# Sparse attention into a two-layer network: the local scores of batches 4 to 7 as one group in six PSUM banks

## The chip, the cores and the metric

The kernel runs on one core of a Trainium2 chip. The metric is device time in microseconds, the median of several executions. Five engines matter here: TensorE (PE, matrix products and transposes into PSUM), ScalarE (ACT: exponentials, relu, copies out of PSUM), VectorE (DVE: masks, squares, normalising), GpSimd (POOL, which here mostly issues loads that cast from fp32 to bf16) and SyncE (SP, which issues the output DMAs and the transposes done by DMA).

## The reference

Attention over 8 batches, 8 heads, 576 positions and 64 channels, with two masks, followed by a network of two layers on all 4608 tokens:

```
mask_local   = (rel >= 0) & (rel < 32)                              # heads 0 to 3
mask_strided = (rel >= 0) & (pos[None, :] % 32 == pos[:, None] % 32) # heads 4 to 7
scores = where(masks, q @ k.T / sqrt(64), -1e9)
attn   = softmax(scores);  x = (attn @ v) as 4608 tokens x 512
out    = relu(x @ w_in) ** 2 @ w_out        # 512 -> 2048 -> 512
```

## The kernel before, in words

**The dense part** is a list of 288 groups of four TensorE products with 512 columns each. The tokens are cut into 9 chunks of 512, and chunk c has groups 32c to 32c+31. The first 16 groups of a chunk are the first layer (`mm1`, L671): ACT's relu takes each result out of PSUM (L685), and DVE squares it (L686). The other 16 are the second layer (`mm2`, L690): four groups fill one output block y, ACT copies it out (L705), and SP sends it. In chunk 0 the second layer goes through w_out quarter by quarter, and its four blocks stay open side by side.

**The attention** is woven between the groups by hand. `PLAN` is a table: a line `n: words` says which steps are issued just before group n (L909 on). Each engine works through its own instructions in the order in which they were issued, so the table sets the order on every engine. Units are numbered u = 4 x batch + pair of heads; units 4b and 4b+1 are the local heads of batch b. The steps that matter below:

- `Su` (`step_S`, L470): the scores of local unit u, 12 small products of 64 rows by 96 columns, in pairs for the two heads of the unit (rows 0 to 63 and 64 to 127 of the array). They fill four half banks of PSUM with 288 columns each, and ACT takes four exponentials of them (L516). With `!` the exponentials are issued at once; otherwise they are spread over the following groups by `later`. DVE then multiplies by the mask (L522).
- `Du.p` (`step_D`, L630): the weighted sums of head p of unit u, six products, then a reciprocal and a multiplication on DVE (L644, L645).
- `Eu` (`step_E`, L649): puts the result x of unit u in its transposed place in `xt`, the input of the first layer. For batches 0 and 1 it uses six TensorE transposes (L661) and a copy (L664) by ACT (`a`) or DVE (`v`); from batch 2 on SP does it with a DMA (L654).
- `sb.p` and `xb.p` (`step_SS`, L539; `step_XX`, L552): part p (0, 1, 2) of the scores and of the products of the strided heads of batch b. An x step takes two banks: one for the sums (L557), of which ACT takes Ln and Exp (L562, L563), and one for the product (L560), which DVE multiplies into `xt` (six instructions at L570 for parts 0 and 1, four at L576 for part 2).
- `Cbq`, `Cbk` load the rows of the strided heads (L354, POOL), `Xbq`, `Xbk` transpose them by DMA (L359, SP), and `kb..` (L370, L373) and `Bb..` (L402) spread keys and values into block form on DVE.
- `Quk`, `Quq` load the rows of a local unit (L283, POOL), `Yu` transposes them by DMA (L383, SP: queries `qT`, then keys `kTl`), `Vb` and `Ub` load values (POOL). In batches 2 and 3 the local queries and keys are cast (`c..`) and transposed by TensorE (`T..`).

**PSUM** has eight banks. Two (`ph`) take the first layer and the second layer of all chunks but the first. One (`py`) is used by chunk 0 alone. Five (`pt`) form a ring that the attention steps take in turn: `bank("pt")` pops the first and puts it at the end. A step that is handed a bank must wait until its last user's result has been read. During groups 19 to 31 one of the five is lent to an output block of chunk 0.

```
    banks = {"ph": [all_banks[i] for i in (4, 5)], "py": [all_banks[2]],
             "pt": [all_banks[i] for i in (6, 7, 0, 1, 3)]}
...
        t = banks[nm].pop(0)
        banks[nm].append(t)
```

Of the kernel before, what the change touches and what calls it, by code (L numbers as in the profile page):

```python
# [9 lines left out]
BF16 = mybir.dt.bfloat16  # L10
AF = mybir.ActivationFunctionType
ALU = mybir.AluOpType
# [28 lines left out]
22: l3k12+13 s1.2  # L41
23: D5.1 x1.0
24: E4a
25: E5a x1.1
26: X2k l3q12+13
27: x1.2
28: V3
29: c9kv
30: c8qv
31: c8ka c9qv X2q  # L50
# [34 lines left out]
77: s3.2  # L85
80: x3.0 B40v
81: B41v
83: x3.1
89: x3.2
90: k40v  # L90
91: S16! k41v
95: U5 D16.0 D16.1
96: S17
97: Y20
99: X5k
100: C6k
# [5 lines left out]
106: Q25k  # L102
107: B50v
108: s4.2 D17.1 B51v
109: Q24k Q24q
111: E17
113: k50v
114: k51v
116: x4.0
119: x4.1  # L110
124: V6
125: x4.2
128: U6 S20!
130: S21
133: D20.0
134: Y24 D20.1 X6k
135: E20 X6q s5.0 C7q Q28k
# [4 lines left out]
141: B60v  # L122
142: E21
143: B61v
148: x5.0
150: x5.1 k60v
152: k61v
153: x5.2
155: S24!
156: V7  # L130
157: U7
161: S25
162: D24.0
165: s6.0 D24.1
166: s6.1
167: X7q
171: X7k
172: B70v
173: Y28 B71v
174: E24 D25.0 D25.1  # L140
175: x6.0 Y29
178: E25
179: s6.2
182: x6.1
186: x6.2
188: k70v
189: k71v
191: S28!
192: S29
197: s7.0  # L150
198: D28.0 s7.1
199: D29.0
# [10 lines left out]
def kernel(  # L163
# [9 lines left out]
    nc = tc.nc  # L173
    B, H, S, D = q.shape
# [4 lines left out]
    scale = 1.0 / (D ** 0.5)  # L179
    QL = 96  # L180
    NL = S // QL
# [12 lines left out]
    singles = ctx.enter_context(tc.tile_pool(name="singles", bufs=1))  # L194
# [15 lines left out]
    banks = {"ph": [all_banks[i] for i in (4, 5)], "py": [all_banks[2]],  # L210
             "pt": [all_banks[i] for i in (6, 7, 0, 1, 3)]}
    places = []

    def bank(nm):
        if places:
            return all_banks[places.pop(0)]
        t = banks[nm].pop(0)
        banks[nm].append(t)
        while id(t) in unread:
            run_due(lambda x: x[1] == unread[id(t)])  # L220
        return t
# [13 lines left out]
    mask_all = singles.tile([128, NL, QL], BF16)  # L235
# [7 lines left out]
    mask_bd = singles.tile([128, 1, W3], BF16)  # L243
    str_rows_t = {nm: singles.tile([SR, RW], BF16, name=f"{nm}_t") for nm in "qk"}
    kTl = [singles.tile([128, 32 + S], BF16, name=f"kTl{i}") for i in range(NV)]
    es = [singles.tile([128, 1280], BF16, name=f"e{i}") for i in range(4)]
    xt = [singles.tile([128, T], BF16, name=f"xt{p}") for p in range(4)]
    w_in_b = singles.tile([128, 4, d_ff], BF16)
    w_out_b = singles.tile([128, 16, d_model], BF16)
# [14 lines left out]
    st = {}  # L264
# [34 lines left out]
    def cast_qk_local(u, name, copy):  # L299
        s = st[u]  # L300
        t = qk_in.tile([QL, 6, 2, D], BF16, name=f"{name}_l")
        copy(t.rearrange("p j h d -> p h j d"), s[name + "f"].rearrange("p h (j d) -> p h j d", j=6))
        s[name] = t
# [62 lines left out]
    def step_K(b, par, copy):  # L366
        o = str_T[b, "k"]
        r = slice(64 * par, 64 * par + 64)
        kb = kbds[b % 2][r, :, 64 * par:64 * par + W3]
        copy(kb[:, 0:NP2], o[r, 0:NP2, 0:W3])  # L370
        src = o[r, :, W3:SP_]
        src = bass.AP(src.tensor, src.offset, [src.ap[0], [SR, NG + 1], [NG * SR, 3], [1, NA]])
        copy(kb[:, NP2:NB].rearrange("c n (g m) -> c n g m", g=3), src)  # L373
# [64 lines left out]
    def later(n, fn, key=None):  # L438
        pending.append((clock[0] + n, key, fn))

    def run_due(test):
        due = [x for x in pending if test(x)]
        for x in due:
            pending.remove(x)
        for x in sorted(due, key=lambda x: x[0]):
            x[2]()
# [5 lines left out]
    def step_T(u, name, copy):  # L452
        s = st[u]
        src = s[name].rearrange("p j h d -> p (j h d)")
        pt = bank("pt").bitcast(BF16)[:, 0:S]
        for j in range(6):
            nc.tensor.transpose(pt[:, QL * j:QL * (j + 1)], src[:, 128 * j:128 * (j + 1)],  # L457
                                ident[0:QL, 0:QL])
        if name == "k":
            full = kTl[v_slot(u)]  # L460
            dst = full[:, 32:32 + S]
        else:
            full = dst = qkT.tile([128, S], BF16, name="qT")
        copy(dst.rearrange("c (p j) -> c p j", j=6), pt.rearrange("c (j p) -> c p j", j=6))
        s[name + "T"] = full
# [4 lines left out]
    def step_S(u, mode=0, halves=range(2)):  # L470
# [48 lines left out]
        def masks(row):  # L519
            x = e[0:kn, S * row:S * (row + 1)].rearrange("p (t c) -> p t c", c=w)  # L520
            m = mask_all if local else mask_str.to_broadcast([kn, n, w])
            nc.vector.tensor_tensor(x, x, m, op=ALU.mult)  # L522
# [10 lines left out]
        later(3, lambda: expo(1, 1), u)  # L533
        later(4, lambda: masks(1), u)

    def blocks(part):
        return range(NJ * part, min(NJ * (part + 1), NB))

# [89 lines left out]
                                r.to_broadcast([QL, 2, NL, D]), op=ALU.mult)  # L628

    def step_D(u, part):  # L630
        run_due(lambda x: x[1] == u)
        s = st[u]
        e = s["e"]
        rhs = s["v"].rearrange("p h t d -> p (h t) d")
        po = bank("pt")[:, 0:NL * (D + 1)].rearrange("p (n d) -> p n d", d=D + 1)
        for n in range(NL):
            c = QL * (NL * part + n)
            m = QL if (part, n) == (0, NL - 1) else 128
            nc.tensor.matmul(po[0:m, n, :], e[:, c:c + m], rhs[:, NL * part + n, 0:D + 1], start=True, stop=True)  # L639
        if part == 0:  # L640
            s["x"] = xl_pool.tile([QL, 2 * NL, D], BF16, name="x_l")
        x = s["x"].rearrange("p (t h) d -> p h t d", h=2)[:, part]
        rinv = small.tile([128, NL, 1], FP32, name="rinv")
        nc.vector.reciprocal(rinv[0:QL], po[0:QL, :, D:D + 1])  # L644
        nc.vector.tensor_tensor(x, po[0:QL, :, 0:D], rinv[0:QL].to_broadcast([QL, NL, D]), op=ALU.mult)  # L645
# [66 lines left out]
    A, V, G = nc.scalar.copy, nc.vector.tensor_copy, nc.gpsimd.tensor_copy  # L712
# [19 lines left out]
    def warm(n):  # L732
        if n:
            pw = bank("py")
            for _ in range(n):
                nc.tensor.matmul(pw, idle[:, 0:128], idle, start=True, stop=True)
# [7 lines left out]
    def run_step(word):  # L744
        word, _, at = word.partition("/")
        places[:] = [int(x) for x in at.split(",") if x]
        op, arg = word[0], word[1:]
        if op == "w":
            warm(int(arg))
        elif op == "c":  # L750
            cast_qk_local(int(arg[:-2]), arg[-2], ENG[arg[-1]])
        elif op == "T":
            step_T(int(arg[:-2]), arg[-2], ENG[arg[-1]])
        elif op == "W":
            step_TS(int(arg[0]), arg[1], int(arg[2]), ENG[arg[3]])
        elif op == "S":
            u, _, half = arg.rstrip("!").partition(".")
            step_S(int(u), int("!" in arg), [int(half)] if half else range(2))
        elif op == "N":
            step_N(int(arg))  # L760
        elif op == "O":
            step_O(int(arg))
        elif op in "sx":
            (step_SS if op == "s" else step_XX)(*(int(x) for x in arg.split(".")))
        elif op == "k":
            step_K(int(arg[0]), int(arg[1]), ENG[arg[2]])
        elif op == "m":
            memset_later(arg[:-1], nc.gpsimd if arg[-1] == "g" else nc.vector)
        elif op == "D":
            if "." in arg:  # L770
                u, part = arg.split(".")
                step_D(int(u), int(part))
            else:
                step_D0(int(arg))
        elif op == "E":
            step_E(int(arg.rstrip("av")), ENG.get(arg[-1]))
        elif op == "P":
            first_part([int(x) for x in arg])
        elif op == "H":
            shift_v_local(int(arg[:-1]), ENG[arg[-1]])  # L780
        elif op == "C":
            load_str_tall(int(arg[:-1]), arg[-1])
        elif op == "Q":
            load_qk_rows(int(arg[:-1]), arg[-1])
        elif op == "X":
            transpose_str(int(arg[:-1]), arg[-1])
        elif op == "Y":
            transpose_local(int(arg))
        elif op == "V":
            load_v_local_all(int(arg))  # L790
        elif op == "U":
            load_v_str(int(arg))
        elif op == "B":
            spread_v_str(int(arg[0]), int(arg[1]), ENG[arg[2]])
        elif op == "l":
            load_qk_local_sw(int(arg[0]), [int(x) for x in arg[2:].split("+")], arg[1])
        elif op == "r":
            load_str_rows(int(arg[0]), arg[1])
        elif op == "i":
            load_w_in(int(arg))  # L800
        elif op == "o":
            load_w_out(int(arg))
        elif op == "z":
            late_constants()
        else:
            raise ValueError(word)
# [99 lines left out]
    for line in PLAN.strip().splitlines():  # L906
        n, words = line.split(":")
        plan.setdefault(int(n), []).extend(words.split())
    for n, g in enumerate(groups):  # L909
        for word in plan.get(n, ()):  # L910
            run_step(word)
        g()
        tick()
# [32 lines left out]
```

## Time and profile before

| | us |
|---|---|
| median of 3 runs | 302.91 (302.55 to 303.26) |
| the profiled execution | 302.61 |
| its span, first to last instruction | 300.9 |
| TensorE matmuls busy | 291.6 |
| VectorE busy | 178.6 |
| ScalarE busy | 173.2 |

Times of events are microseconds from the start of the span. A "busy" TensorE is not TensorE at its peak: products overlap, so one product of 512 columns is listed with 379 ns, but four in a row take 0.86 us. Some records of products are missing, so counts such as x15 can stand for 16. The granted clock of TensorE is 1.000 over the whole span. "L560 <- L570" in a wait means that line 560's instruction waited for line 570's. A DMA's time to landing is counted from its issue.

### The profile page before, as it was taken

The page shows a single profiled execution, that of the slowest core. Times are in us where ns is not written, and L with a number is a line of the kernel's source. Part 1 is how long each engine was busy: PE and PEld are TensorE (multiplying, and loading weights), DVE is VectorE, ACT ScalarE, POOL GpSimd, SP SyncE. Part 2 cuts the span into 40 slices and gives each one's busy share as a digit, 9 for nine tenths or more (in the row PEclk, how much of TensorE's full clock was granted, in tenths as well). Part 3 has the DMA queues.
Part 4 walks back from the last instruction along what each step waited for, and adds up shares of the span by engine and source line. Part 5 has one row for each costly group of instructions (what it writes and reads, how often), then busy time and mean ns, then how long its engine had stood idle before and what let it go on. Part 6 is the DMA issues. An engine that isn't in the chain of part 4 may idle for free.

```text
span 300.9 us, 5686 instructions
## 1 busy us (share of the span) xinstructions
PE 291.6 (97%) x2141; PEld 146.2 (49%) x2179; DVE 178.6 (59%) x459; ACT 173.2 (58%) x332; POOL 72.1 (24%) x105
## 2 busy tenths in 40 slices
PE   7989998999999999999999999999999999999996
PEld 3644554545545444444454445444454444444444
DVE  5776688588679677585467485666575524104400
ACT  3777855786668734874387447643875356226611
POOL 8755932007204009064302820000000000000000
PEclk9999999999999999999999999999999999999999
DMA  7999999997999999999998999511011110010012
GB/s 153 179 207 202 189 203 190 166 215 114 142 169 158 149 155 197 150 160 119 208 157 153 151 195 164 84 55 71 35 23 25 68 68 1 35 72 35 0 70 72
DMA packets 93643, 37.28 MB, mean 124 GB/s; under 512 B 78956, under 2 KB 87750, under 8 KB 93616
## 3 DMA queue, kind: packets, MB, share of 16 engines
q0 software_dynamic: 54960, 18.82, 59.2%
q1 hardware_dynamic: 38512, 18.03, 32.4%
q8 instruction: 17, 0.28, 0.4%
q10 hardware_dynamic: 144, 0.07, 0.1%
q14 instruction: 10, 0.08, 0.1%
HBM read 38.21 MB, written 9.44 MB: 158 GB/s over the span
## 4 chain that ended last, share of the span: by engine, by line
PE 84%; DMA 9%; POOL 3%; issue 2%; DVE 1%; ACT 0%; DVEq 0%; POOLq 0%
PE psb L701 38%; PE psb L679 37%; DMA w_in_b<-in_moe_w_in_dram 5%; DMA w_out_b<-in_moe_w_out_dram 4%; PE psb L639 2%; PE psb L500 1%; PE psb L560 1%; PE psb L546 1%; PE psb L726 1%; PE psb L557 1%; DVE xt L570 1%; POOL w_in_b L429 1%; PE psb L457 1%; POOL xt L295 0%; POOL vl L423 0%
## 5 line engine op out<-in xcount | busy, mean ns | idle before, releaser
L679 PE MATMUL psb<-xt,w_in_b 128*128 128x512 bf16 x557 | 131.8, 379 | 1.3 <-DMA w_in_b<-in_moe_w_in_dram 0.2
L701 PE MATMUL psb<-w_out_b,g_sb 128*128 128x512 bf16 x542 | 126.1, 379 | 1.4 <-issue 0.5
L685 ACT ACTIVATE r<-psb 128x512 bf16<-128x512 f32 x144 | 85.9, 599 | 34.2 <-PE psb L679 31.0
L686 DVE TENSOR_TENSOR g_sb<-r 128x512 bf16<-128x512 bf16 x144 | 60.3, 424 | 65.2 <-ACT r L685 64.5
L679 PEld LDWEIGHTS <-w_in_b 128*128 128x128 bf16 x576 | 53.1, 98 | 58.7 <-issue 1.0
L701 PEld LDWEIGHTS <-g_sb 128*128 128x128 bf16 x560 | 51.7, 97 | 57.5 <-DVE g_sb L686 0.5
L705 ACT COPY y<-psb 128x512 f32<-128x512 f32 x35 | 20.6, 590 | 53.2 <-PE psb L701 50.4
L570 DVE TENSOR_TENSOR xt<-psb,rv 64x144 bf16<-64x144 f32 x84 | 33.9, 404 | 18.2 <-ACT rv L563 17.1
L516 ACT ACTIVATE e<-psb 128x288 bf16<-128x288 f32 x56 | 19.9, 416 | 6.7 <-PE psb L500 6.7
L562 ACT ACTIVATE rv<-psb 128x432 f32<-128x432 f32 (+1 forms) x21 | 10.5, 502 | 12.2 <-PE psb L557 12.2
L576 DVE TENSOR_TENSOR xt<-psb,rv 64x270 bf16<-64x270 f32 (+1 forms) x28 | 10.9, 432 | 8.8 <-ACT rv L563 8.6
L645 DVE TENSOR_TENSOR x_l<-psb,rinv 96x384 bf16<-96x384 f32 x28 | 15.5, 553 | 1.0
L522 DVE TENSOR_TENSOR e<-e,mask_all 128x576 bf16<-128x576 bf16 x28 | 12.4, 452 | 3.8 <-ACT e L516 3.5
L547 ACT ACTIVATE e<-psb 128x432 bf16<-128x432 f32 (+1 forms) x21 | 10.4, 496 | 6.0 <-PE psb L546 6.0
L354 POOL DMA_DIRECT2D q_t<-in_q_dram x6 | 3.4, 575 | 41.8 <-DMA qT_s<-q_t 27.8
L423 POOL DMA_DIRECT2D vl<-in_v_dram x7 | 10.0, 1435 | 10.7 <-DMA vl<-in_v_dram 6.7
L283 POOL DMA_DIRECT2D q_l<-in_q_dram x16 | 11.6, 732 | 3.9 <-DMA k_t<-in_k_dram 1.9
L283 POOL DMA_DIRECT2D k_l<-in_k_dram x16 | 11.8, 741 | 2.7 <-DMA k_t<-in_k_dram 1.4
L563 ACT ACTIVATE rv<-rv 128x432 f32<-128x432 f32 (+1 forms) x21 | 11.2, 533 | 0.7
L639 PEld LDWEIGHTS <-e 128*128 128x128 bf16 x168 | 8.4, 100 | 4.8
L354 POOL DMA_DIRECT2D k_t<-in_k_dram x6 | 3.3, 546 | 27.5 <-DMA kT_s<-k_t 27.2
L560 PEld LDWEIGHTS <-vb 128*128 128x128 bf16 x154 | 7.1, 97 | 5.0 <-issue 1.3
(114 smaller groups left out, 209.2 us busy)
## 6 DMA issues: line engine op xcount, KB each, us to landing
out_dram<-y SPq DMA_DIRECT2D x35, 256.0 KB, 4.4
vl<-in_v_dram POOLq DMA_DIRECT2D x7, 384.0 KB, 12.2
w_in_b<-in_moe_w_in_dram POOLq DMA_DIRECT2D x4, 512.0 KB, 12.3
w_out_b<-in_moe_w_out_dram POOLq DMA_DIRECT2D x4, 512.0 KB, 13.3
q_t<-in_q_dram POOLq DMA_DIRECT2D x7, 288.0 KB, 5.8
k_t<-in_k_dram POOLq DMA_DIRECT2D x7, 288.0 KB, 7.1
v_st<-in_v_dram POOLq DMA_DIRECT2D x7, 216.0 KB, 8.4
k_l<-in_k_dram POOLq DMA_DIRECT2D x16, 72.0 KB, 8.7
```

The source lines that it names most:

```text
L283: nc.gpsimd.dma_start(out=t[:, :, hh, :], in_=src[b, 2 * p + hh].rearrange("(t p) d -> p t d", p=QL))
L516: nc.scalar.activation(e[0:kn, lo:lo + S // 2], pss[row][half][0:kn, 0:S // 2], AF.Exp, scale=scale)
L522: nc.vector.tensor_tensor(x, x, m, op=ALU.mult)
L563: nc.scalar.activation(rv, rv, AF.Exp, scale=-1.0)
L570: nc.vector.tensor_tensor(to[:, :, NJ * part:NJ * (part + 1), par], of, by, op=ALU.mult)
L639: nc.tensor.matmul(po[0:m, n, :], e[:, c:c + m], rhs[:, NL * part + n, 0:D + 1], start=True, stop=True)
L645: nc.vector.tensor_tensor(x, po[0:QL, :, 0:D], rinv[0:QL].to_broadcast([QL, NL, D]), op=ALU.mult)
L679: nc.tensor.matmul(ph, w_in_b[:, kk, 128 * ff:128 * (ff + 1)], xt[kk][:, 512 * c:512 * (c + 1)], start=(kk == order[0]), stop=(kk == order ...
L685: nc.scalar.activation(r, ph, AF.Relu)
L686: later(1, lambda: nc.vector.tensor_tensor(g[:, ff, :], r, r, op=ALU.mult))
L701: nc.tensor.matmul(py, g[:, ff, 128 * j:128 * (j + 1)], w_out_b[:, ff, :], start=(ff == 0), stop=(ff == 15))
L705: nc.scalar.copy(y, py)
```

## The change

1. **Early.** `E5a`, the transposition of x of unit 5 (batch 1) with ACT's copy, is issued before group 28 instead of group 25, after `V3`. Before group 25 then stands `x1.1` alone.
2. **Six banks.** From group 32 on, the bank of `py` joins the ring of the attention steps, which then has six.
3. **Batches 4 to 7.** A new step `Gb` takes the place of the two steps `S(4b)` and `S(4b+1)`. It issues the 24 score products of both local units in one go, into six banks with 384 columns each (three banks for either head of the pair), and at once six exponentials of 384 columns. The four masks follow two and three groups later. The two tiles `e0` and `e1` become halves of one tile, ordered by head, then unit. `G4` to `G7` stand before groups 90, 121, 154 and 188, all in the second layer of a chunk; the S steps stood before 91 and 96, 128 and 130, 155 and 161, 191 and 192.
4. **Strided products.** The x steps of batches 3 to 6 move so that they are done before the G step: x3.1 and x3.2 from 83 and 89 to 82 and 85; x4 from 116, 119, 125 to 109, 112, 116; x5 from 148, 150, 153 to 144, 146, 149; s6.2 from 179 to 169; x6.1 and x6.2 from 182 and 186 to 179 and 183.
5. **D** reads the new order, and its last weights of part 1 are 96 columns wide instead of 128 in batches 4 to 7.

```diff
-25: E5a x1.1
+25: x1.1
 26: X2k l3q12+13
 27: x1.2
-28: V3
+28: V3 E5a
...
-83: x3.1
-89: x3.2
-90: k40v
-91: S16! k41v
+82: x3.1
+85: x3.2
+90: G4 k40v
+91: k41v
 95: U5 D16.0 D16.1
-96: S17
...
-109: Q24k Q24q
+109: Q24k Q24q x4.0
 111: E17
+112: x4.1
...
-116: x4.0
-119: x4.1
+116: x4.2
+121: G5
 124: V6
-125: x4.2
-128: U6 S20!
-130: S21
+128: U6
...
-148: x5.0
-150: x5.1 k60v
+144: x5.0
+146: x5.1
+149: x5.2
+150: k60v
 152: k61v
-153: x5.2
-155: S24!
+154: G6
...
-161: S25
...
+169: s6.2
...
-179: s6.2
-182: x6.1
-186: x6.2
-188: k70v
+179: x6.1
+183: x6.2
+188: G7 k70v
 189: k71v
-191: S28!
-192: S29
...
-    es = [singles.tile([128, 1280], BF16, name=f"e{i}") for i in range(4)]
+    es01 = singles.tile([128, 2560], BF16, name="e01")
+    es = [es01[:, 0:1280], es01[:, 1280:2560]] + [singles.tile([128, 1280], BF16, name=f"e{i}") for i in (2, 3)]
...
+    def step_G(b):
+
+        us = (4 * b, 4 * b + 1)
+        bk = [bank("pt") for _ in range(6)]
+        bk = [bk[0::2], bk[1::2]]
+        for t in range(2 * NL):
+            for row in range(2):
+                s, j = st[us[t // NL]], t % NL
+                rows, c = slice(64 * row, 64 * row + 64), QL * (t % 4)
+                nc.tensor.matmul(bk[row][t // 4][:, c:c + QL], s["kT"][rows, QL * j:QL * j + 128],
+                                 s["qT"][rows, QL * j:QL * (j + 1)], start=True, stop=True)
+        e = es01[:, 0:4 * S].rearrange("p (r c) -> p r c", r=2)
+
+        def masks(row):
+            x = e[:, row].rearrange("p (u t c) -> p u t c", u=2, c=QL)
+            for i in range(2):
+                nc.vector.tensor_tensor(x[:, i], x[:, i], mask_all, op=ALU.mult)
+
+        for row in range(2):
+            for i in range(3):
+                nc.scalar.activation(e[:, row, 4 * QL * i:4 * QL * (i + 1)], bk[row][i][:, 0:4 * QL], AF.Exp, scale=scale)
+            later(row + 2, lambda row=row: masks(row), ("G", b, row))
...
     def step_D(u, part):
-        run_due(lambda x: x[1] == u)
+        run_due(lambda x: x[1] in (u, ("G", u // 4, part)))
         s = st[u]
-        e = s["e"]
+        e = es01[:, 2 * S * part + S * (u % 4):] if u > 15 else es[u % 4][:, S * part:]
...
-            c = QL * (NL * part + n)
-            m = QL if (part, n) == (0, NL - 1) else 128
+            c = QL * n
+            m = QL if n == NL - 1 and (u > 15 or part == 0) else 128
...
+        if n == 32:
+            banks["pt"] += banks.pop("py")
```

More of the change, by code (lines that the diff above doesn't have):

```diff
@@ L758, in run_step @@
             step_S(int(u), int("!" in arg), [int(half)] if half else range(2))
+        elif op == "G":
+            step_G(int(arg))
         elif op == "N":
```

## The prediction

> **What bounds the kernel now.** I read the page's first part, then the waits, then the chain that ended last cut into stretches, then the timeline around the steps that move, and the DMA issues last. The page:
>
> ```profile
> PE 291.6 (97%) x2141; PEld 146.2 (49%) x2179; DVE 178.6 (59%) x459; ACT 173.2 (58%) x332; POOL 72.1 (24%) x105
> ...
> PE 84%; DMA 9%; POOL 3%; issue 2%; DVE 1%; ACT 0%; DVEq 0%; POOLq 0%
> ```
>
> TensorE sets the end, and ACT and DVE have room on the average. From about 50 us to the end the chain is TensorE alone, so only two things can shorten the kernel: less TensorE time per step, or a TensorE wait taken away. The waits hold one that matters after the start:
>
> ```profile
> PE psb L560 <- DVE xt L570: 1.1, 1, 1.1
> ```
>
> The timeline shows where (columns: start, duration, engine and line; in brackets the idle time before it):
>
> ```profile
> 45.04 2.49 DVE L570 TENSOR_TENSOR xt<-psb,rv 64x144 bf16<-64x144 f32 x6 [0.56 <-ACT rv L563]
> ...
> 45.88 0.42 PE L661 MATMUL psb<-ident,x_l 96*128 96x96 bf16 x6
> ...
> 46.14 0.35 PE L557 MATMUL psb<-e,ones_bd 128*128 128x432 bf16 x1
> ...
> 47.58 0.38 PE L560 MATMUL psb<-e,vb 128*128 128x54 bf16 x8 [1.09 <-DVE xt L570]
> ```
>
> This is x1.1. Its product needs a PSUM bank, and the next in the ring of four (one of five is lent to y) is the one that x1.0's six DVE multiplications read until 47.53.
>
> The price of a score step is in the chain (step 16 at 114.25, four groups, then D of unit 16) and in the timeline:
>
> ```profile
> 114.25 0.36 PE psb L500 x12
> 114.61 0.16 issue
> 114.77 3.40 PE psb L701 x15
> 118.17 0.38 PE psb L639 x12
> ```
>
> ```profile
> 114.18 0.43 PE L500 MATMUL psb<-qT,kTl 64*128 64x96 bf16 x12
> ```
>
> From 114.25 to 118.17 are 3.92 us. Four groups take 4 x 0.863 = 3.45 (x4 matmuls show as 0.86), so a score step costs 0.46 us. Its 12 matmuls take 0.43 from first start to last end, and one alone 0.20 (page group of L500: 205 ns): 11 intervals in 0.23, 0.021 each. So 0.25 is matmuls and 0.21 is paid once per visit.
>
> **The change, part by part.** Times below are those of the profiled execution: 302.61 us, of which the span is 300.9; the median of the three runs is 302.91, 0.3 above it.
>
> *E5a from group 25 to 28.* One bank less is taken between x1.0 and x1.1, so x1.1's product gets the bank of x1.0's normaliser, which ACT has read by 44.42. The bank read until 47.53 goes to x1.2. Laid out from the rows: group 24 ends at 45.87, x1.1 takes 0.39 (0.18 + 0.21, as at 76.67), groups 25 and 26 1.73, so x1.2 is reached at 47.99, after 47.53. With x1.2 0.30, group 27 0.86 and E5a's six transposes 0.26, group 28 starts at 49.41, where it now starts at 49.98 + 0.86 = 50.84: 1.43 us earlier. Cover: group 28 needs the last quarter of w_out, which POOL's wait of 1.81 us shows landed before 47.03. x_l of unit 5 is ready at 44.47. ACT's copy (0.64) then ends near 50.3 and x1.2's DVE work near 51.6, where chunk 1 begins at 52.9. Without E5a ahead, ACT takes x1.1's Ln sooner. POOL's V3 is issued ahead of it, and SP has nothing of it. The next late thing is k20v, whose transposed rows land at 62.9 whatever TensorE does (X2k leaves at 54.81 when its load lands, 8.1 us to landing). DVE then idles some 2.2 us instead of 0.78. The masks for D8.0 end at 65.25, and TensorE would be there at 65.2, so 0.1 is lost. Gain kept: 1.3.
>
> *Scores as one group.* 24 matmuls in one visit cost 24 x 0.021 + 0.21 = 0.70 against 2 x 0.46 = 0.92: 0.22 less, four times 0.88. The Trainium skill, "TensorE: Matmul & The Clock Gate" (section "Wait — 56ns, not 53.3ns?"), has starts never under 25 ns apart; by it the second dozen costs 0.30 instead of 0.25, and the sum would lose 0.2. The trace's 21 ns speak against that, so I keep 0.25.
>
> ACT: six exponentials of 384 columns for eight of 288. 288 take 0.416 and 512 take 0.599 (relu), so 384 about 0.49, and back to back (four of 288 in 1.32, 0.33 each) about 0.41: 2.5 us at one time. They lie in the second layer, where ACT has a copy of 0.59 per 3.45 us; a y copy behind them ends over 1 us before its bank is taken again. The masks stay four per batch.
>
> *Banks.* From group 32 the ring has six, and a G step takes all. Before G4 the last user is x3.2 (group 85): DVE, with x3.0, x3.1, B40 and B41 ahead of it (2.45 + 1.05 + 2.45 + 1.57), is done some 9.2 us after group 80, and G4 is reached after ten groups and three x steps, 9.7. Before G6 and G7 the same count leaves 0.8 to 1.5. Before G5 DVE is tightest: x4.0, three squares, x4.1, k50, k51 and x4.2 add to 8.9 us from about 134.8 minus the shift, and end within 0.3 us of need.
>
> *x4.0 into the first layer (group 109).* Its Ln and Exp (0.53 + 0.56) delay a relu by 1.1 us. Two ph banks leave 0.26 (0.863 - 0.599) plus the 0.39 of x4.0 itself: bound 0 and 0.5, I take 0.3 at group 111. x5 stays in the second layer.
>
> *D.* The last weights of part 1 are 96 columns wide instead of 128. Part 0, which has this already, shows 0.20 against 0.18: 0.02 x 8 = 0.16.
>
> *What G asks earlier.* G5 at group 121 needs unit 21's keys, which S21 needed only at group 130. SP sends them late (first fence), and the DMA issues give the time to landing (second):
>
> ```profile
> 128.96 2.02 SPq L654 DMA_TRANSPOSE xt<-x_l  x1
> 131.08 1.97 SPq L383 DMA_TRANSPOSE qT<-q_l  x1
> 133.15 2.58 SPq L383 DMA_TRANSPOSE kTl<-k_l  x1
> ```
>
> ```profile
> kTl<-k_l SPq DMA_TRANSPOSE x1, 11.6
> ```
>
> They land at 133.15 + 11.6 = 144.75. Group 121 now starts at 143.20 (x4.1 ends at 141.47, two groups). With the change G5 is reached at 143.20 - 1.3 - 0.22 + 0.30 (x4.2 now ahead) + 0.3 + 0.04 = 142.3, its unit-20 half ends at 142.6, and the rest waits 2.1 us, less d, by which the transposes come earlier. This is the term that decides.
>
> d: the queue from 122 to 135 is SP back to back. It starts when Q20's load lands, which waits for the batch-4 key rows, and those for batch 3's:
>
> ```profile
> 90.80 0.60 POOL L354 DMA_DIRECT2D k_t<-in_k_dram  x1 [10.73 <-DMA kT_s<-k_t]
> ```
>
> ```profile
> 72.94 1.71 SPq L654 DMA_TRANSPOSE xt<-x_l  x1
> 75.59 0.33 SPq L709 DMA_DIRECT2D out_dram<-y  x1
> 76.03 3.93 SPq L359 DMA_TRANSPOSE qT_s<-q_t  x1
> ```
>
> The last three go out as TensorE's results come (x_l ready 72.91, y at 75.57), so they move up by about 1.3; the loads on POOL before them (q_t at 68.31) do not. Hence d lies between 0 and 1.3. From 70 to 74 the hardware queue had only 10 to 15% of the engines' time beside POOL's 84 to 98%, yet 68 to 70 was two thirds idle and a transpose sent at 68.5 would use that; so I take 0.85, nearer the upper end. The Trainium skill, "DMA: Bandwidth & Descriptors" (the paragraph on arbitration), says that each engine takes turns between queues packet by packet; by it alone the earlier transposes keep their whole lead, and d would be 1.3.
>
> For G4 the keys of unit 16 land at 105.09 + 5.9 = 111.0 and it is reached near 112.1. For G6 and G7 the last keys land 9 and 11 us ahead. V6, U6, k50, k51, k60 and E17, which the moved steps pass, wait for nothing of theirs that is late: POOL at V6 waits for an earlier load, SP at E17 is behind its own queue.
>
> **Sum.** -1.3 (x1.1) - 0.88 (scores) + 0.16 (D) + 0.3 (x4.0) + (2.13 - 0.85) (G5) = -0.44. On the profiled execution 302.17, on the median 302.5.
>
> **The rivals.**
> (1) No wait at G5: the DMAs lie otherwise and the keys land 2.1 us or more before 144.75. Then the sum is -1.72, 301.2. For it: the landing time of 11.6 us is the longest of the eight kTl transposes (median 4.7), so a little less crowding is enough. Against it: what crowds them (V5, C6q and the Q25 loads, 130 to 135) belongs to the same chain and moves with it.
> (2) Slower: the chain of loads does not move, or the six-bank DVE chain and DMA crowding push the keys later. G5 then pins everything before it, and the early gain is worth nothing. The sum is -0.44 + (0.85 - d). With d = 0 that is +0.41, 303.3; the kernel is slower than now once the keys land after 144.34, and by over 0.6 us after 144.95. For it: the root loads are DMA-bound already (POOL waits 27 us for these transposes in all). Against it: SP's three rows above.
> (3) The x copy brings nothing because x1.1 only meets another wait. The rows exclude it up to group 32, and if G5 waits anyway, it changes only d: as (2).
>
> **Chances.** 0.2% is 0.6 us, about what a measurement of this kernel can tell from no change. Forecast with a wait at G5 of 0.6 to 1.8 us: 0.55 (within 0.2% 0.38, faster 0.17); its own range is 301.9 to 303.0. Rival 1: 0.25, all faster. Rivals 2 and 3: 0.20, slower 0.17 and 0.03 within. So faster 0.42, same 0.41, slower 0.17. The range goes from rival 1's 301.2 to 303.5, which is rival 2 with d = 0 and 0.2 for the run-to-run spread (302.55 to 303.26).
>
> **What would show it.** Right: no wait of L560 for L570 near 46; group 28 near 49.4; 24 L500 matmuls in about 0.68 us from first start to last end; a wait of L500 or its weights for a DMA near 143, ended by kTl; an x4.0 with a relu late by a microsecond near 131; fewer exponentials in the first layer. Wrong: G5 without idle time ahead of it (rival 1), the transposes of unit 21 at 133 as now (rival 2), or an idle TensorE before G4, G6 or G7, where DVE would still hold a bank.

## The result, and the profile after

| | before | changed |
|---|---|---|
| median, us (6 runs each) | 303.18 (302.55 to 303.81) | 301.67 (300.85 to 302.02) |
| ratio, 95% interval | | 0.9946 (0.993 to 0.9963) |
| the profiled execution, us | 302.61 | 301.85 |
| its span, us | 300.9 | 300.1 |

The changed kernel is faster by about half a per cent, 1.5 us between the medians. That is inside the predicted range and clear of 0.2%, but it is not the case that the forecast thought likeliest. No wait at G5 shows, and that was the condition of rival 1 (a gain of 1.72). Here and below, medians and ranges are over all executions, while a ratio leaves out those more than 1.5% above the fastest of their kernel.

The page of the changed kernel, first part and shares of the chain:

```profile
PE 291.2 (97%) x2142; PEld 146.7 (49%) x2179; DVE 178.8 (60%) x459; ACT 173.0 (58%) x324; POOL 72.4 (24%) x105
...
PE 84%; DMA 10%; POOL 2%; issue 2%; ACT 1%; DVE 0%; DVEq 0%; POOLq 0%; ACTq 0%
```

TensorE still sets the end, with the same products; ACT has eight instructions less (24 exponentials for 32). The timeline around x1.1:

```profile
46.26 5.05 DVE L590 TENSOR_TENSOR xt<-psb,rv 64x144 bf16<-64x144 f32 x12 [0.56 <-ACT rv L583]
...
47.10 0.35 PE L577 MATMUL psb<-e,ones_bd 128*128 128x432 bf16 x1
...
47.28 0.38 PE L580 MATMUL psb<-e,vb 128*128 128x54 bf16 x8
```

The product of x1.1 (L580, formerly L560) follows its sums without the idle 1.09 us. The multiplications of x1.0 and x1.1 now run as one stretch of twelve.

In this execution the second quarter of w_out landed late, so group 20 starts at 41.40 instead of 40.17. By group 32 it has caught up (54.26 against 54.29): the stretch from group 20 to 32 takes 12.86 us instead of 14.12, which is 1.26 saved. From group 32 to the last block (L746, formerly L726) it takes 239.45 instead of 240.15, another 0.70. The sum, 1.96, less the late start of 1.23, is the 0.73 by which the two traces differ. The early loads vary between executions of one kernel, so single traces must be compared by stretches and not by their ends.

The chain around the grouped scores of batch 5, and the timeline of the same place:

```profile
143.50 0.62 PE psb L542 x24
144.12 0.16 issue
144.28 5.99 PE psb L721 x27
150.27 4.32 PE psb L699 x20
```

```profile
143.43 0.54 PEld L542 LDWEIGHTS <-kTl 64*128 64x128 bf16 x24 [0.42 <-issue]
143.43 0.69 PE L542 MATMUL psb<-qT,kTl 64*128 64x96 bf16 x24
```

All 24 products run through with no wait for a DMA. From 143.50 to 150.27 are 6.77 us; seven groups take 6.04, so a grouped score step costs 0.73. Its six exponentials take 2.40 us, where 2.5 was predicted. SP and the DMA issues of this trace show why nothing waits:

```profile
133.45 1.22 SPq L380 DMA_TRANSPOSE qT<-q_l  x1
134.77 1.21 SPq L380 DMA_TRANSPOSE kTl<-k_l  x1
```

```profile
kTl<-k_l SPq DMA_TRANSPOSE x1, 5.3
```

The keys of unit 21 are sent 1.6 us later than before the change, and land 4.7 us earlier: 134.77 + 5.3 = 140.07, against 144.75. Unit 21's products come some 0.25 us (12 x 0.021) after G5 is reached, at 143.75, so the keys are 3.7 us early.

### The profile page after: what moved, and what is told of

It reads as the page before. It is cut to its first block, busy times and chain, and to the rows that moved or that the text cites. A ratio compares the mean times of both kernels' runs of the same rounds, so it can differ in the third digit from the quotient of the medians.

```text
span 300.1 us, 5660 instructions
## 1 busy us (share of the span) xinstructions
PE 291.2 (97%) x2142; PEld 146.7 (49%) x2179; DVE 178.8 (60%) x459; ACT 173.0 (58%) x324; POOL 72.4 (24%) x105
## 4 chain that ended last, share of the span: by engine, by line
PE 84%; DMA 10%; POOL 2%; issue 2%; ACT 1%; DVE 0%; DVEq 0%; POOLq 0%; ACTq 0%
PE psb L721 39%; PE psb L699 36%; DMA xt<-in_q_dram 6%; DMA w_out_b<-in_moe_w_out_dram 4%; PE psb L659 2%; PE psb L580 1%; PE psb L566 1%; PE psb L746 1%; PE psb L577 1%; POOL w_in_b L426 1%; PE psb L542 1%; PE psb L454 1%; PE psb L497 0%; POOL xt L292 0%; POOL vl L405 0%
## 5 line engine op out<-in xcount | busy, mean ns | idle before, releaser
L582 ACT ACTIVATE rv<-psb 128x432 f32<-128x432 f32 (+1 forms) x21 | 10.5, 500 | 10.4 <-PE psb L577 10.4
L567 ACT ACTIVATE e<-psb 128x432 bf16<-128x432 f32 (+1 forms) x21 | 10.4, 496 | 4.3 <-PE psb L566 4.3
L553 ACT ACTIVATE e<-psb 128x384 bf16<-128x384 f32 x24 | 9.6, 509 | 3.4 <-PE psb L542 3.4
L549 DVE TENSOR_TENSOR e<-e,mask_all 128x576 bf16<-128x576 bf16 x16 | 6.7, 458 | 6.9 <-ACT e L553 6.9
L659 PE MATMUL psb<-vl,e 128*128 128x65 bf16 x168 | 9.5, 195 | 0.0
```

The source lines that it names most:

```text
L582: nc.scalar.activation(rv, pn, AF.Ln)
```

## The experiments

A run's ratio is to the kernel before, timed beside it; it is compared with the changed kernel by the difference of the two ratios. Theory A, formed from the traces above: the gain is x1.1's bank wait (1.3) and four merged visits (0.84), less x4.0's stall (0.2) and D (0.16), and G5 finds its keys there. Rivals: the early gain is taken back by transposes that land when they land (B); the sixth bank by itself is what helps (C); only the place of the scores counts, not the merging (D).

**e1: the x copy alone.**

```diff
-25: E5a x1.1
+25: x1.1
-28: V3
+28: V3 E5a
```

> The kernel before with one edit: E5a stands before group 28, behind V3, instead of before group 25. Theory A (the wait of x1.1 for its PSUM bank is real TensorE time, and nothing takes it back): 1.2 to 1.4 us faster than before, ratio near 0.9957, and no wait of the strided product for the six multiplications near 46 us. Theory B (the gain is taken back, because the transposed key rows of batch 2 and later ones land when they land): within 0.4 us of before, and the lost time shows as DVE or TensorE idle near 63 or 90 us.

Measured: 301.85 against 303.25, ratio 0.9965 (0.9947 to 0.9983). That is 1.06 us faster by the ratio, 0.5 to 1.6. The wait for L570 is gone from the trace, and the stretch from group 20 to 32 takes 12.87 us, as in the changed kernel (14.12 before). A holds; B, a gain of at most 0.4, lies outside the interval. The value is a little under A's 1.2 to 1.4, which the interval includes.

**e2: the sixth bank alone.**

```diff
     for n, g in enumerate(groups):
+        if n == 32:
+            banks["pt"] += banks.pop("py")
```

> The kernel before with one edit: from group 32 on the ring of the attention steps has six banks. Theory A (past 50 us no TensorE wait for a bank is left to remove): within 0.3 us of before. Theory C (the sixth bank by itself is what shortens the kernel): 0.8 us or more faster.

Measured: 303.43 against 303.25, ratio 1.0019 (0.9997 to 1.0041), not to be told from no change. C falls: past group 32 the waits before hold none for a bank, so there was none to remove, and the stretch from group 32 to the last block takes 240.17 us (240.15 before). The sixth bank is only what makes the grouped step possible.

**e3: the changed kernel with E5a back at 25.**

```diff
-25: x1.1
+25: E5a x1.1
-28: V3 E5a
+28: V3
```

> The changed kernel with E5a back before group 25. Theory A: the wait of 1.1 us for the bank near 46 us is back, and the kernel is 1.2 to 1.4 us slower than the changed one, so 0 to 0.5 us faster than before (ratio 0.998 to 1.000). Theory C (the gain comes from the grouped scores, the sixth bank and the earlier strided products): it keeps at least 1 us of the 1.5, ratio 0.995 to 0.997.

Measured: 303.05, ratio 0.9989 (0.9969 to 1.0009): not to be told from before, 1.3 us slower than the changed kernel by the ratios. The waits of its trace have the old one back, and one more that e1 and the changed kernel's first trace do not have:

```profile
PE psb L580 <- DVE xt L590: 1.1, 1, 1.1
PE psb L497 <- DVE qT L461: 0.8, 1, 0.8
```

So the x copy carries most of the gain from either side, and the time of e3 alone doesn't show that the rest of the change gains anything; e4 comes to that. What the second line means comes with e9.

**e4: two visits in place of one.**

```diff
-90: G4 k40v
+90: S16! k40v
 91: k41v
+92: S17!
...
-121: G5
+121: S20!
+123: S21!
```

and so for batches 6 and 7, with the old `step_D`; sixth bank, early E5a and moved x steps as in the changed kernel.

> The changed kernel's table with two score steps in place of each grouped one (the first where G stood, the second two groups later, each in four half banks with four exponentials of 288 columns), and D as before the change. It has the sixth bank, the early E5a and the moved strided products. Theory A (one visit of 24 products is cheaper than two of 12 by 0.14 to 0.22 us): 0.5 to 0.9 us slower than the changed kernel, about 0.7 us faster than before, ratio near 0.9977. Theory D (the visit's fixed price is hidden, and only the place of the scores counts): as fast as the changed kernel, ratio near 0.9946.

Measured: 301.99, ratio 0.9974 (0.9956 to 0.9991): 0.8 us slower than the changed kernel by the ratios, as A has it. The two intervals overlap, so the time alone does not exclude D. A stretch of the traces does. From D13.0 (group 73) to D29.1 (group 204) TensorE does the scores of batches 4 to 7, and the waits for late first loads lie ahead of it. The first and last line of the stretch, for the kernel before, the changed one and e4:

```profile
97.08 0.38 PE psb L639 x12
...
224.09 0.18 PE psb L639 x6
```

```profile
97.05 0.38 PE psb L659 x12
...
223.35 0.20 PE psb L659 x6
```

```profile
96.40 0.38 PE psb L638 x12
...
223.45 0.18 PE psb L638 x6
```

The stretch takes 127.01 us before and 126.30 in the changed kernel. It takes 127.05 in e4, which has every part of the change except the grouping and the wider weights of D. Over all traces it is 127.01 to 127.05 without the grouped steps (before, e1, e2, e4) and 126.30 to 126.31 with them (changed, e3, e8 to e11); e5 and e6, below, have a wait of their own in it. So the grouping is worth 0.75 us with D's wider weights paid for, and D falls. The new places of the strided products and the sixth bank bring nothing by themselves in this stretch, on balance.

**e5: x4 out of the first layer.**

```diff
-109: Q24k Q24q x4.0
+109: Q24k Q24q
-112: x4.1
+112: x4.0
...
-114: k51v
+114: x4.1 k51v
-116: x4.2
+117: x4.2
```

> The changed kernel with the three strided products of batch 4 before groups 112, 114 and 117 instead of 109, 112 and 116, so that none lies in the first layer. Theory A (Ln and Exp of x4.0 hold a relu back by a microsecond, and TensorE idles about 0.2 to 0.3 us at group 111): 0.1 to 0.3 us faster than the changed kernel, ratio to before 0.9938 or so, and the relu of group 109 starts as its product ends. Rival (VectorE then still holds the last two banks when G5 wants them): a wait of the grouped scores near 143 us, 0.2 to 0.5 us slower than the changed kernel.

Measured: 301.91, ratio 0.9961 (0.9934 to 0.9987): no difference from the changed kernel that can be told. Its trace shows both halves at once: the relu stall is gone (the four groups from 108 on run through in 3.47 us), and the wait that the rival named stands in its place:

```profile
PE psb L542 <- DVE xt L596: 0.2, 1, 0.2
```

G5 waits 0.2 for the bank that x4.2's multiplications still read. What is saved at group 111 is paid at 121: from D13.0 to D29.1 the trace takes 126.43 us, 0.13 more than the changed kernel.

**e6 and e7: the keys of unit 21 later.** Y21 goes from before group 104 to before 112 (e6, shown) or to a line of its own before 120 (e7).

```diff
-104: Y21 s4.1
+104: s4.1
-112: x4.1
+112: Y21 x4.1
```

> The changed kernel with the DMA transposes of unit 21 (Y21) issued before group 112, behind E17 on SP, instead of before group 104. If the keys land with the slack that the changed kernel's trace shows (140.07 against a need at 143.75), issuing them some 1.3 to 2.6 us later still costs nothing: the same time as the changed kernel, ratio near 0.9946. If the landing is tight in most executions, up to 1 us slower than the changed kernel.

> The changed kernel with Y21 issued before group 120, so on SP behind the first two output blocks of chunk 3. The keys then leave near 143.5 and land near 149, some 5 us after G5 wants them. If a late landing costs TensorE one for one, as the prediction had it for the changed kernel: 4 to 6 us slower than the changed kernel, ratio to before 1.008 to 1.015, with an idle time of that size ahead of the scores of unit 21 in the trace. If TensorE can make up for it: less than 2 us.

Measured, e6: median 304.71, 12 runs from 301.83 to 309.62; before 303.11. The ratio of 1.0015 (0.999 to 1.004) is without the four longest, which belong to what this run is about, so I go by the median: 1.6 us above before, and so some 2.5 to 3 us slower than the changed kernel. I had expected nothing, or 1 us. That the longer executions are longer by the wait at G5 is likely but not shown, as none of them has a trace. The traced execution was the fastest of the twelve, and even it waits at G5:

```profile
142.81 0.43 PE L542 MATMUL psb<-qT,kTl 64*128 64x96 bf16 x12
...
143.66 0.28 PEld L542 LDWEIGHTS <-kTl 64*128 64x128 bf16 x12 [0.57 <-DMA kTl<-k_l]
143.66 0.43 PE L542 MATMUL psb<-qT,kTl 64*128 64x96 bf16 x12 [0.43 <-DMA kTl<-k_l]
```

The step breaks in the middle, after unit 20's twelve products, as the prediction had drawn it for the changed kernel. The expectation had the size of the delay wrong: it put the request 1.3 to 2.6 us later. In SP's queue of this trace the keys stand behind the two x copies E16 and E17 (7.36 us until both are sent), and leave 14.4 us after those of unit 20 (121.52), where it is 9.3 in the changed kernel and 9.6 before, so some 5 us later against the chain:

```profile
126.53 7.36 SPq L674 DMA_TRANSPOSE xt<-x_l  x2
...
135.93 1.28 SPq L380 DMA_TRANSPOSE kTl<-k_l  x1
```

Measured, e7: 314.95, ratio 1.0348 (1.0298 to 1.0397), 13 us slower than the changed kernel, where I had expected 4 to 6. The late landing is paid in full, but its size was wrong again (sent at 144.96, landed 11 us later):

```profile
143.27 0.43 PE L543 MATMUL psb<-qT,kTl 64*128 64x96 bf16 x12
...
155.97 0.66 PE L543 MATMUL psb<-qT,kTl 64*128 64x96 bf16 x12 [12.27 <-DMA kTl<-k_l]
```

On top of the 12.3 us comes a slower clock. The busy time by stretches shows it around the wait (the third figure from the end is the mean granted clock of the stretch: 1.00, 0.62, 0.58, 1.00):

```profile
130.00:143.00 13.00, 12.88 (x91) 6.29 (x89) 11.61 (x31) 7.28 (x15) 9.47 (x12) 1.00 1.58 138
143.00:156.00 13.00, 0.73 (x16) 0.32 (x16) 0.00 (x0) 0.59 (x2) 1.42 (x3) 0.62 1.59 136
156.90:160.40 3.50, 3.43 (x10) 1.34 (x10) 1.65 (x4) 1.46 (x4) 0.00 (x0) 0.58 0.02 5
160.40:164.00 3.60, 3.60 (x19) 1.60 (x18) 0.00 (x0) 0.59 (x1) 0.00 (x0) 1.00 0.19 73
```

The means 0.62 and 0.58 mix two values. In shorter stretches of the same trace the granted clock is 1.00 from 144 to 146, 0.50 from 147 to 159 and 1.00 from 160 on; the stretches in between (0.58 from 146 to 147, 0.60 from 159 to 160) put the changes at about 146.2 and 159.8. From group 32 to the last block this trace takes 253.71 us, 14.26 more than the changed kernel: 12.27 of wait, and about 1.9 for 3.8 us of products at half the clock.

Both together show that the mechanism of the forecast's deciding term is real. The changed kernel escapes it, with 3.7 us to spare in its first trace and less than 0.5 in e9's, below.

**e8: batch 2's strided keys spread later.**

```diff
-39: k20v
-41: S8! k21v
+41: S8!
...
-45: D8.1
+45: D8.1 k20v
+46: k21v
```

> The changed kernel with the spreading of batch 2's strided keys (k20v, k21v) before groups 45 and 46 instead of 39 and 41, so that VectorE no longer stands in front of the DMA transposes that land at 62 to 66 us. Theory A (part of the early gain is given back there, 0 to 0.9 us by how late the loads of that execution are): 0.1 to 0.6 us faster than the changed kernel, ratio to before 0.9930 to 0.9943, and no VectorE wait of over 0.5 us for that DMA. Rival (the wait is hidden as a rule): the same time as the changed kernel.

Measured: 302.19, ratio 0.9967 (0.9946 to 0.9987): no gain. The wait of VectorE in front of the transposed rows is only handed on: the strided scores of batch 2, at group 48, now wait for the late spreading.

```profile
PE psb L567 <- DVE kb L368: 0.7, 1, 0.7
```

**e9: the changed kernel again; e10: the keys of unit 21 sent ahead of E16.**

```diff
-102: Q25q V5 E16
+102: Q25q V5 Y21 E16
 103: C6q s4.0
-104: Y21 s4.1
+104: s4.1
```

> The changed kernel itself, timed once more beside the kernel before and beside the next run. Theory A (the wait at G5 does not occur in most executions): ratio 0.993 to 0.9965, no wait of the grouped scores for a DMA in the trace. Rival (its six executions so far missed a tail): a median of 1 us or more above 301.67, with single executions of 304 and more.

> The changed kernel with Y21 issued before E16 on SP instead of behind it, so that the keys of unit 21 leave some 2 us earlier. Theory A: the same time as the changed kernel within 0.3 us, since there is nothing left to gain at G5. Rival (G5 still waits for the keys in a good part of the executions): 0.4 us or more faster than the changed kernel, with fewer slow executions.

Measured, e9: 302.18 (300.58 to 305.26), ratio 0.9955 (0.993 to 0.9981). The first ratio is confirmed. The spread is wider than the six runs had shown: two of the twelve are above 304, as the rival had it, but the median is only 0.5 above 301.67. e10: 301.32, ratio 0.9946 (0.9927 to 0.9965), not to be told from e9. In e9's trace the keys land at 134.52 + 10.4 = 144.92 and G5 is reached at 145.07; there is no wait here, but TensorE itself was late. At G5's time of the first trace, 143.50, unit 21's products would have stood about 1.2 us, if the keys had landed no sooner. Why it was late:

```profile
59.47 0.52 DVE L399 COPY vb<-v_st 54x1408 bf16<-54x1408 bf16 x1 [2.17 <-DMA v_st<-in_v_dram]
...
64.17 0.43 PE L497 MATMUL psb<-qT,kTl 64*128 64x96 bf16 x12 [1.15 <-DVE qT L461]
```

VectorE stands 2.17 us in front of B20v, whose values have not landed. The copies of unit 8's transposes (L461) are queued behind it, and the scores of unit 8 wait 1.15 for them. This is the same line as e3's second. From group 32 to D13.0 this trace takes 44.14 us, 1.35 more than the first one (42.79).

**e11: e10 with those values spread later.**

```diff
-34: C3q B20v
-35: T8kv B21v
+34: C3q
+35: T8kv
+43: B20v
 45: D8.1
+46: B21v
```

> The kernel of the run before (Y21 ahead of E16), with batch 2's strided values spread before groups 43 and 46 (B20v, B21v) instead of 34 and 35. In the traces whose first loads landed late, VectorE stood up to 2.2 us in front of B20v, with the copies of unit 8's transposed queries and keys behind it, and the scores of unit 8 waited about 1.1 us for them. Theory A (that is where late executions give back the early gain): no wait of the scores of unit 8 for VectorE in the trace, and 0.2 to 0.6 us faster than the run before, ratio to before 0.992 to 0.994. Rival (what VectorE no longer waits for there, it waits for at k20v, whose rows land at 62 to 66 us, and D8.0 waits behind that): no difference that can be told from the run before.

Measured: 301.18 (300.59 to 302.31, 6 runs), ratio 0.9921 (0.9903 to 0.994). By the estimate this is the fastest of all and clearly ahead of before, but its interval overlaps e10's and the changed kernel's, so what B20v's move alone is worth stays open. Its trace shows both expectations partly right: no wait of unit 8's scores, but VectorE now stands 2.90 us at k20v, and D8.0 waits for a mask behind it:

```profile
PE psb L661 <- DVE e L521: 0.8, 1, 0.8
```

**What stays open: what sets the landing time of unit 21's keys.** Over twelve traces, sent and landed:

| trace | keys sent | V5's values sent | to landing | landed |
|---|---|---|---|---|
| before | 133.15 | 132.32 | 11.6 | 144.75 |
| changed | 134.77 | 135.90 | 5.3 | 140.07 |
| e1 | 133.86 | 133.17 | 7.9 | 141.76 |
| e2 | 134.72 | 134.08 | 7.5 | 142.22 |
| e3 | 136.80 | 137.97 | 6.0 | 142.80 |
| e4 | 130.83 | 130.69 | 7.7 | 138.53 |
| e5 | 132.78 | 131.81 | 8.5 | 141.28 |
| e6 (Y21 later) | 135.93 | 129.73 | 7.7 | 143.63 |
| e8 | 132.15 | 131.93 | 7.5 | 139.65 |
| e9 | 134.52 | 133.29 | 10.4 | 144.92 |
| e10 | 131.64 | 132.38 | 6.3 | 137.94 |
| e11 | 130.11 | 130.84 | 7.5 | 137.61 |

Where the 384 KB of V5 leave after the keys, it takes 5.3 to 7.5 us; where they leave before, 7.5 to 11.6, longest where they lead by 0.8 to 1.2. One and the same kernel shows both (changed 5.3, e9 10.4). That fits transfers taking turns on the same engines, which is what the Trainium skill, "DMA: Bandwidth & Descriptors" (the paragraph on arbitration), describes. No run changed this order alone, so it is an association over traces and not shown.

## Why the prediction was right or wrong

- **Range and sign of the sum: right.** 301.67 lies in 301.2 to 303.5. The point, 302.5, was 0.8 too high, and the likeliest case (a wait at G5 of 0.6 to 1.8, given 0.55) did not occur. Rival 1, given 0.25, did: its sum of 1.72 is near the measured 1.5. The range held because it was stretched to that rival, not because the point's own sum was right.
- **The step that failed** is the term (2.13 - 0.85) at G5. It measured 0. None of the five traces that have both G5 and Y21 where the changed kernel has them (changed, e3, e5, e8, e9) waits for the keys. The term was built on one landing time, 11.6 us, and on the assumption that the crowding which made it so long travels with the chain. The changed kernel's landing took 5.3, and over the twelve traces above 11.6 is the longest. The rows before the change had the warning, and rival 1 used it: the median of the eight kTl transposes was 4.7. The shift d was wrong too (the keys were sent 1.6 later, not 0.85 earlier), probably because this execution's loads began late; that weighed less than the landing, 6.3 shorter. The mechanism is right: e6 and e7 make the wait appear at the place drawn. The term would have had to be a spread over landings, with about 0 as its likeliest value. Part of the outcome is luck of the landing: with e9's, and TensorE on time, the wait would have been about 1.2 us, if the keys had landed no sooner, which is the size that was forecast. What makes a landing long stays open, as said above.
- **The x copy: right.** Group 28 is reached 9.40 us after group 20 instead of 10.67, 1.27 earlier where the rows gave 1.43; e1 measured 1.06 (0.5 to 1.6). "0.1 lost at k20v" was too small for some executions: from group 32 to D13.0 the traces take 42.79 to 44.14 us (42.79 before), so 0 to 1.35 is lost there, and B20v, which the prediction did not name, is the first place where VectorE stops.
- **The grouped scores: right to 0.02.** Predicted 0.70 a visit, measured 0.72 to 0.73. The stretch from D13.0 to D29.1 agrees: 0.75 less than in e4, plus the 0.14 that seven wider D cost there, is 0.89, or 0.22 a visit as predicted. 24 products take 0.69 from first start to last end: 23 intervals of 21 ns. The 25 ns that the Trainium skill's page "TensorE: Matmul & The Clock Gate" gives do not hold for these pairs on the two halves of the array. By the stretches, batch 5's part gained 0.43 (from D16.0 to D20.0, 36.62 to 36.19). The prices give the same: three S steps at 0.467 less G5's 0.73, less x4.0's stall and two D, 0.40.
- **x4.0: right.** Group 108 starts at 130.96 and x4.1 at 135.03, 4.07; four groups and x4.0 take 3.84. The stall is 0.23, predicted 0.3. The chain of the changed kernel passes through ACT there:

```profile
132.91 0.02 ACT rv L583
...
133.38 0.59 ACT r L705
```

- **D: right.** Both parts now show 0.20, as in 0.39 for twelve products at 118.39 (0.38 before).
- **Banks before G: right.** No grouped step of the changed kernel waits for one. The tight one was G5, as said; in e5, which moves x4.2 by one group, it does wait, 0.2.
- **Not seen:** about 0.2 us between x6.0 and the scores of batch 7. There the step s6.2 used to stand just before a group whose last product waited for a square on VectorE. With x6.1 there instead the square is done in time.

The terms as measured, 1.27 + 4 x 0.21 - 0.23 - 0.16 + 0.2, give 1.9, as the two stretches of the traces do (1.96). The runs show 1.5 (1.1 to 2.1 by the interval). The loss at B20v and k20v in some executions has the size of the difference, but it was not measured over many executions.

## What to carry to other kernels

A step that asks for data earlier must be costed against the spread of that data's landing, not against the landing in one trace; the request needs slack of the size of that spread, because here some 5 us of delay in the queue put the median up by 2.5 to 3. More slack than that need not pay: sending the keys some 2 us sooner (e10) brought nothing that could be told. Where TensorE is saturated, look for the few waits in which one step holds a ring's bank for the next: one allocation less between them was worth more (1.26 us in the traces) than four merged score steps (0.75). An engine that is queued behind a late load hands its wait to whatever stands behind it, so moving one such step only pays if the next one is not late too.

## What the runs showed of the hardware that I had not expected

- The landing of the same DMA transpose, of the same size and at the same place in the table, varied from 5.3 to 11.6 us over the nine traces that have it there (all of the table but e6, e10 and e11).
- In e7's wait of 12.3 us the granted clock fell from 1.00 to 0.50 at about 146.2, 2.5 us after the last product had ended (143.27 + 0.43). It was back at 1.00 at about 159.8, 3.8 us after the products had resumed; in between they came 0.43 apart instead of 0.216. The wait of 1.09 us before the change had no such effect, with a granted clock of 1.00 over its stretch. The Trainium skill, "TensorE: Matmul & The Clock Gate" (the table of the two states), has half rate after an idle window of about 3.4 us and full rate after a busy one. The trace agrees on the two rates and nearly on the return, but here half rate came after 2.5 us without a product.
- A visit of small products on two halves of the array costs about 0.21 us beside the products themselves, whether 12 or 24 (0.46 - 12 x 0.021, and 0.73 - 24 x 0.021 = 0.23).
